# Gated mix of linear attention and a gated MLP: denominators in 128 rows, one output tile turned in place, weights and operands asked for at other points

## Chip, cores, metric

The kernel runs on one core of a Trainium2 chip. The metric is the device time of one execution in microseconds, the median of several runs. The core has five engines with instruction queues of their own: TensorE (PE; its weight loads are listed as PEld), VectorE (DVE), ScalarE (ACT), GpSimd (POOL) and SyncE (SP), which here only issues DMAs. ScalarE and GpSimd can issue DMAs too.

## What is computed

```python
x = A_x                                              # 1 x 2048 x 576
g = sigmoid((x * gate_w).sum(-1, keepdims=True))
# a: linear attention, 32 heads of 18
q, k, v = split(x @ wqkv)
phi_q = concat(softmax(q @ w_phi), softmax(-(q @ w_phi)))     # per head, 36 features
phi_k = the same of k
num = phi_q @ (phi_k^T v);  den = phi_q . sum(phi_k) + 1e-6
a = (num / den) @ wo
# b: gated MLP, 576 -> 4608 -> 576
b = (relu(x @ W_gate) * (x @ W_up)) @ W_down
out = g * a + (1 - g) * b
```

Everything is float32. Most products are done in three passes of a rounded type, high x high, high x low and low x high, so nearly every operand is split by ScalarE (the high part, a copy) and VectorE (the low part, a subtraction).

## The kernel before

The 2048 rows are 16 tiles of 128 (`t`), or 4 blocks of 512 (`TB`), handled in the order `BLOCKS` = 3, 0, 1, 2. So "block 0" of the text below is the first handled, and "block 3" holds tiles 8 to 11. The program is one function, `gated_mix_kernel`, with three stages.

1. Tiles: for each tile keys, queries, values and their softmax parts; `kv_step` sums keys times values. The softmax parts `e` of the queries are turned by TensorE (`turn_all`, L374) into 108-row operands. Tiles of the last block go straight into their operand buffer `PH`; the others are stored to a DRAM scratch `eT` and fetched a block at a time (`fetch`, L431). At the very start the loop at L219 loads five slices of `x` and `wv`.
2. Division and projection, a block `b` at a time: `sums(b, ...)` multiplies `PH` by the keys' sums (L556), ScalarE copies numerators to `R` and small DMAs gather denominators in `dn`; `invert(b)` takes the reciprocal times the gate and sends it by DMA to rows of `kt_`; `split_inverse(b)` splits it on GpSimd into `rd`; `divide(b, k)` spreads it over the rows of a head by a matmul with a 0/1 matrix (`spread`, L616), multiplies `R` and splits the result into `oh`, `ol`; `first_out` (block 0) or `project_out(b, m)` multiplies by `wo`, and `rows_out` stores to the DRAM scratch `att`. `dn`, `R` and the chain invert, DMA, split, divide exist once per block.
3. Main stage: 72 units (two halves of the rows, 36 column chunks of the MLP's weights), each of seven products (`product`, L1098) by a Strassen-like scheme. Operands `XO` are split copies of sums of `x`; each unit's weights are split by `blocks`, `sums_of_blocks`, `block_sums` in the first half and reloaded from DRAM in the second (`load_operands`, L883). The down products add into `ac` tiles that begin with `att` (`load_acc`), and are stored at the half's end (`store`, L1182). Around units 35 to 37 the operands are exchanged (`swap_in`).

`in_order` fixes the order of instructions on the engines it names to that of the program: TensorE, SyncE and GpSimd in stage 2, all engines in stage 3. In stage 2 a scheduler places VectorE's and ScalarE's instructions, apart from those inside `after(...)` or `behind()`, which must follow the ones named. A wait at the head of SyncE's or GpSimd's queue therefore holds all DMAs behind it.

Of the kernel before, what the change touches and what calls it, by code (L numbers as in the profile page):

```python
# [83 lines left out]
def gated_mix_kernel(  # L84
# [126 lines left out]
    with tc.tile_pool(name="ps_v", bufs=1, space=PSUM) as ps_v:  # L211
        pv = [[ps_v.tile([P, TB], F32, name=f"pv{2 * i + c}")[:, :VC[c][1]] for c in range(2)] for i in range(4)]

        warm = raw.tile([P, TB], F32R, name="warm", tag="raw")
        nc.vector.memset(warm.bitcast(F32), 0.0)
        for n in range(15):
            nc.tensor.matmul(pv[3][1], warm[:, :P], warm[:, :VC[1][1]], start=True, stop=True)
        xh, xl, x4 = x_tiles(0)
        for k in range(5):  # L219
            w = raw.tile([P, TB + VW], F32, name="xwv", tag="raw")  # L220
            nc.sync.dma_start(w[:, :TB], xT[:, k, :TB])
            nc.sync.dma_start(w[:, TB:], wv[:, k])
            if k < 4:
                split(xh[:, k], xl[:, k], w[:, :TB])
            else:
                split_x4(x4, w[:, :TB])
            split(wv_h[:, k, :VW], wv_l[:, k, :VW], w[:, TB:])
            for i in range(4):
                ts = slice(i * P, (i + 1) * P)
                for c, (v0, vn) in enumerate(VC):  # L230
                    cs = slice(v0, v0 + vn)
                    if k < 4:
                        ops = [(xh[:, k, ts], wv_h), (xh[:, k, ts], wv_l), (xl[:, k, ts], wv_h)]
                    else:
                        ops = [(x4[:, ts], wv_h), (x4[:, ts], wv_l)]
                    for n, (m, w_) in enumerate(ops):
                        nc.tensor.matmul(pv[i][c], m, w_[:, k, cs], start=k == 0 and n == 0,  # L237
                                         stop=k == 4 and n == 1)
# [131 lines left out]
    def turn_all(t, bb):  # L370
# [55 lines left out]

    def fetch(tb, queue=nc.sync):
        operands(tb)
        for i in range(4):
            t = 4 * tb + i  # L430
# [136 lines left out]

    RD, OW = [], {}

# [20 lines left out]
    def invert(b):  # L590
# [3 lines left out]
        tt(out=dn, in0=gT[:, BLOCKS[b] * P:(BLOCKS[b] + 1) * P], in1=dn, op=MULT)  # L594
        nc.sync.dma_start(kt_[2 * H * (b % 2):][:H, :TB], dn)

    def split_inverse(b):

        if not RD:
            RD.append(rb.tile([4 * H, TB], F32R, name="rd", bufs=1))  # L600
        i = 2 * H * (b % 2)
        d2, hi, lo = kt_[i:i + H, :TB], RD[0][i:i + H], RD[0][i + H:i + 2 * H]
        nc.gpsimd.tensor_copy(hi, d2)
        pt(out=lo, in0=d2, in1=hi.bitcast(F32), op=SUB)

    def divide(b, k):
# [7 lines left out]
        ps = kv_bank(1 - k % 2 if b > 1 or b == 1 and k < 2 else 0)  # L614
        half = slice(2 * H * (b % 2), 2 * H * (b % 2 + 1))
        nc.tensor.matmul(ps[:n], spread[half, k, :n], RD[0][half], start=True, stop=True)  # L616
        r = R[:n, k]
# [46 lines left out]
    with in_order(tc, nc, nc.tensor, nc.sync, nc.gpsimd):  # L664
# [75 lines left out]
        gather(1, 3, 2, 1, 0)  # L740
        split_inverse(1)
        with after(tc, nc, nc.vector, halves[1]):
            whole(final)
        first_out(3, range(5))
        two = pp.tile([P, 2, TB], F32, name="po", tag="pp")
        turn_all(FIRST - 1, [(2, turned(kv_bank(0))), (0, turned(two[:, 0])), (1, turned(two[:, 1]))])
        store_turned(FIRST - 1, nc.gpsimd)
        divide(0, 1)
# [4 lines left out]
    xo = ctx.enter_context(tc.tile_pool(name="xo", bufs=3, **L_))  # L753
    xr = ctx.enter_context(tc.tile_pool(name="xr", bufs=2, **L_))
    op_ = BS.enter_context(tc.tile_pool(name="op", bufs=2, **L_))
    tb_ = BS.enter_context(tc.tile_pool(name="tb", bufs=6, **L_))
    XO = {}
    def root_rows(tb):
# [5 lines left out]
    def rows_out(b, m, ps):  # L764
# [70 lines left out]

    RAW, WO = {}, {}
    units = [(0, c) for c in range(NC)] + [(1, (c - 2) % NC) for c in range(NC)]
# [40 lines left out]
    def load_operands(u):  # L878
# [6 lines left out]
        WO[u] = {1: (b, 0), 2: (b, 1), 4: (b, 2), 5: (o, 2), 6: (o, 0), 7: (o, 3), 3: (o, 1)}  # L885

    def early():
        for i in (5, 6):
# [40 lines left out]
    with in_order(tc, nc, nc.tensor, nc.sync, nc.gpsimd):  # L929
        x0, x1, x2 = (operand_ahead(i) for i in range(3))  # L930
        fetch(BLOCKS[3], nc.gpsimd)
        load_operand(0, 0, nc.gpsimd)
        load_operand(0, 1, nc.gpsimd)
        first_out(2, range(5))
        halves = two[:, 0], two[:, 1]
        sums(2, (4, 5), halves)
        divide(0, 0)
        first_out(1, range(5))
        sums(2, (3, 2), halves)
        for m in range(5):  # L940
            first_out(0, (m,))
            rows_out(0, m, PW[m])
            if m in (0, 1, 3):
                divide(1, (4, 3, None, 2)[m])
        sums(2, (1, 0), halves)
        gather(2, 4)
        invert(2)
        gather(2, 3, 2, 1, 0)
        split_inverse(2)
        divide(1, 1)  # L950
        divide(1, 0)
        for m in range(5):
# [4 lines left out]
            if m == 2:  # L957
                gather(3, 4)
                invert(3)
                gather(3, 3, 2, 1, 0)  # L960
                split_inverse(3)
                whole(x0)
            if m > 0:
                divide(2, 5 - m)
            if m in (0, 1):
                root_rows(m + 2)
            if m == 4:
                divide(2, 0)
                whole(x1)
        for m in range(5):  # L970
# [4 lines left out]
            if m == 1:  # L975
# [15 lines left out]
                load_rests(0, (6,))  # L991
        unit0, unit1 = unit(0), unit(1)
        for m in range(5):
            project_out(3, m)
            with behind():
                if m == 0:
                    next(unit0)
                if m == 1:
                    whole(unit0)
                if m == 2:  # L1000
                    next(unit1)
                if m == 3:
                    whole(unit1)
            if m in (1, 2):
# [15 lines left out]

    NG = NC // 2
    DOWN = (1, 5, 6, 3, 7, 2, 4)
    ADDS = {1: (0, 0), 5: (1, 1), 3: (0, 1), 6: (0, 1), 2: (0, 0), 7: (1, 1), 4: (1, 0)}
    WDR, WD, W4, HID, ACC, ACC4, BANK, REST = {}, {}, {}, {}, {}, {}, {}, {}

    def load_down(g):
        if g < 2 * NG:
            WDR[g] = wdp.tile([P, 9 * P], F32, name="wdr", bufs=1)  # L1030
            nc.sync.dma_start(WDR[g], wd[units[2 * g][1] // 2])

# [147 lines left out]
    def store(keys):  # L1180
        for hf, i, m, t in keys:
            nc.sync.dma_start(out[rows(i, m, t, hf)], ACC.pop((hf, i, m, t)))  # L1182
            if hf == 0:
                load_acc(1, i, m, t)

# [38 lines left out]
    def swap_in(u, j):  # L1224

        i = j + 7 * (u - NC + 1)
        if 2 <= i < 7:
            if i in (3, 4):
                load_rests(1, (2, 3, 4) if i == 3 else (5, 6))
            load_in_place(1, i)  # L1230
        if i in (1, 2):
            operand(1, i - 1)
        if 2 <= i - 4 < 7:
            low_in_place(1, i - 4)
        if 2 <= i - 3 < 7:
            high_in_place(1, i - 3)
        if 2 <= i - 5 < 7:
# [3 lines left out]
    done = []  # L1241

    def add_up():

        if PEND:
            done.extend(PEND.pop()())
        store(done)
        done.clear()

# [37 lines left out]
    def step(u, j):  # L1287
# [122 lines left out]
        if u == 0:  # L1410
            if j < 3:
                next(early, None)
            elif j < 5:
                plain_down(0, (high, low)[j - 3])
# [28 lines left out]

    later_half, early = second_half(), early()
    with in_order(tc, nc, nc.tensor, nc.vector, nc.scalar, nc.gpsimd, nc.sync):
        load_down(0)
        load_w(2)
        for u in range(len(units)):
# [89 lines left out]
def _layout(A_x, A_wqkv, A_w_phi, A_wo, B_W_gate, B_W_up, B_W_down, gate_w):  # L1538
# [32 lines left out]
    mask = np.zeros((QK, QG + 4), np.float32)  # L1571
    spread = np.zeros((4, H, 5, P), np.float32)
    for r in range(QK):
        h = r // (2 * DH)
# [3 lines left out]
    for k in range(5):  # L1578
        for r in range(P):
            spread[:, wo_rows[k * P + r] // DH, k, r] = 1.0  # L1580
    spread = spread.reshape(4 * H, 5, P)
# [19 lines left out]
```

## Time and profile before

| | |
|---|---|
| median of 3 runs | 1608.23 us (1607.2 to 1611.56) |
| profiled execution: its own time / span | 1607.92 us / 1605.9 us |
| mean granted TensorE clock | 0.997 |
| TensorE / VectorE / ScalarE / GpSimd busy | 98% / 74% / 35% / 11% |

Stage 2 lies at about 240 to 353 us of the span, the main stage after it; the halves change at about 980. Rows of the profile read: start in us, length in us, engine, line of the kernel, operation, tile written <- tiles read, shape, count, and in brackets the idle time before it with what ended it. "SPq" is SyncE's DMA queue.

### The profile page before, as it was taken

Reading aid. Unit: us, or ns where it says so; the run is one execution under the profiler, and the core shown is the slowest. Engines: PE = TensorE matmul, PEld = TensorE weight load, DVE = VectorE, ACT = ScalarE, POOL = GpSimd, SP = SyncE. Lnnn points to the kernel's source line nnn. Section 1 sums busy time; section 2 is a strip of 40 time slices with the busy share of each in tenths; the row PEclk is TensorE's granted clock in tenths of the full one; section 3 lists DMA queues with packets and bytes.
Section 4 is the critical chain, followed back from the end, with each engine's and each line's share of the span. In section 5 each row is a group of like instructions: output and inputs, shape, how many; then the busy total and the mean of one; then the engine's idle time right before and its main releaser. Section 6 shows DMA issues by size and latency. Waiting matters only on the chain.

```text
span 1605.9 us, 20175 instructions
## 1 busy us (share of the span) xinstructions
PE 1580.5 (98%) x7823; PEld 1314.5 (82%) x7823; DVE 1192.4 (74%) x1864; ACT 559.9 (35%) x918; POOL 171.3 (11%) x234
## 2 busy tenths in 40 slices
PE   9999999899999999999999999999999999999998
PEld 9899995577888888888888887788888888888887
DVE  4997775477787877878777777677776777767777
ACT  4444335463332332333333234223223232232331
POOL 0125522100000000000000002111111111111110
PEclk9999999999999999999999999999999999999999
DMA  5373415569655565655554525634344343443432
GB/s 165 108 242 134 162 41 148 177 234 351 215 220 212 217 249 217 222 218 189 214 197 172 208 83 175 242 129 183 134 151 181 129 174 143 148 184 129 169 148 74
DMA packets 65370, 284.59 MB, mean 177 GB/s; under 512 B 6842, under 2 KB 17338, under 8 KB 56572
## 3 DMA queue, kind: packets, MB, share of 16 engines
q1 hardware_dynamic: 62828, 273.30, 46.8%
q0 software_dynamic: 1872, 8.97, 1.8%
q8 instruction: 61, 1.00, 0.2%
q10 hardware_dynamic: 576, 1.05, 0.2%
q14 instruction: 33, 0.27, 0.0%
HBM read 172.67 MB, written 109.21 MB: 176 GB/s over the span
## 4 chain that ended last, share of the span: by engine, by line
PE 91%; DMA 3%; DVE 3%; ACT 1%; issue 1%; POOL 0%; SPq 0%; ACTq 0%; DVEq 0%; POOLq 0%
PE cx L1098 28%; PE ca L1098 13%; PE pd L1138 12%; PE pd L1161 10%; PE cy L1098 7%; PE kv L175 4%; PE pq L175 3%; PE pk L175 3%; PE pm L1138 2%; PE pm L1161 2%; PE kv L417 1%; DMA dn<-R 1%; PE ptr L374 1%; PE pv L237 1%; DMA wdr<-wd 1%; PE pw L175 1%
## 5 line engine op out<-in xcount | busy, mean ns | idle before, releaser
L1205 ACT ACTIVATE hh<-g 128x512 fp32r<-128x512 f32 x195 | 120.1, 624 | 459.1 <-DVE g L1255 289.8
L1176 DVE TENSOR_TENSOR ac<-pd,ac 128x512 f32<-128x512 f32 x238 | 164.0, 689 | 145.9 <-PE pd L1161 145.7
L1098 PE MATMUL cx<-xo,wb 128*128 128x512 f32 x1008 | 250.9, 392 | 5.0 <-DVE u L1380 3.5
L1098 PE MATMUL cx<-xo,ws 128*128 128x512 f32 x1008 | 252.4, 390 | 3.0 <-ACT g L1259 2.8
L1098 PE MATMUL ca<-xo,ws 128*128 128x512 f32 x1008 | 252.0, 389 | 0.6 <-DMA ws<-wsd 0.6
L1098 PEld LDWEIGHTS cx<-xo,wb 128*128 128x128 f32 x1008 | 189.2, 189 | 47.1 <-DVE u L1380 4.4
L1098 PEld LDWEIGHTS cx<-xo,ws 128*128 128x128 f32 x1008 | 188.9, 188 | 43.8 <-ACT g L1259 4.7
L1098 PEld LDWEIGHTS ca<-xo,ws 128*128 128x128 f32 x1008 | 189.1, 188 | 40.3 <-issue 1.0
L1138 PE MATMUL pd<-hh,wd 128*128 128x512 f32 x576 | 200.7, 389 | 0.0
L1161 PE MATMUL pd<-hh,wd 128*128 128x512 f32 x476 | 185.2, 389 | 0.0
L1144 DVE TENSOR_TENSOR ac<-pd,ac 128x512 f32<-128x512 f32 x144 | 99.1, 688 | 106.6 <-PE pd L1138 103.1
L1210 DVE TENSOR_TENSOR hl<-g,hh 128x512 fp32r<-128x512 f32 x195 | 136.4, 699 | 1.9 <-ACT hh L1205 0.2
L1259 ACT ACTIVATE g<-cx 128x512 f32<-128x512 f32 x144 | 84.9, 590 | 128.1 <-PE cx L1098 128.0
L1138 PEld LDWEIGHTS pd<-hh,wd 128*128 128x128 f32 x576 | 108.1, 188 | 22.6
L1098 PE MATMUL cy<-xo,wb 128*128 128x512 f32 x504 | 125.9, 389 | 0.0
L1061 ACT ACTIVATE wd<-wdr 128x384 fp32r<-128x384 f32 (+1 forms) x106 | 62.3, 606 | 152.9 <-DMA wdr<-wd 152.9
L1138 PE MATMUL pd<-hl,wd 128*128 128x512 f32 x288 | 112.2, 389 | 1.0 <-ACT xo L830 1.0
L1098 PEld LDWEIGHTS cy<-xo,wb 128*128 128x128 f32 x504 | 94.6, 188 | 19.6
L1161 PEld LDWEIGHTS pd<-hh,wd 128*128 128x128 f32 x476 | 89.4, 188 | 18.5
L1161 PE MATMUL pd<-hl,wd 128*128 128x512 f32 x238 | 92.6, 389 | 0.0
L814 POOL TENSOR_TENSOR xo<-xr,xo 32x512 fp32r<-32x512 f32 x5 | 8.2, 1637 | 653.9 <-DVE xo L814 646.1
L1064 DVE TENSOR_TENSOR wd<-wdr,wd 128x384 fp32r<-128x384 f32 (+1 forms) x106 | 69.3, 669 | 5.5 <-ACT wd L1061 5.5
(250 smaller groups left out, 2564.9 us busy)
## 6 DMA issues: line engine op xcount, KB each, us to landing
wsd<-ws SPq DMA_DIRECT2D x34, 1280.0 KB
ws<-wsd SPq DMA_DIRECT2D x34, 1280.0 KB
wbd<-wb SPq DMA_DIRECT2D x34, 960.0 KB
wb<-wbd SPq DMA_DIRECT2D x34, 960.0 KB
wr<-wgu SPq DMA_DIRECT2D x36, 768.0 KB
wdr<-wd SPq DMA_DIRECT2D x36, 576.0 KB
eT<-et SPq DMA_DIRECT2D x10, 594.0 KB
xt<-xb SPq DMA_DIRECT2D x7, 768.0 KB
```

What stands on the lines that cost most here:

```text
L175: nc.tensor.matmul(ps, w, m, start=i == 0, stop=i == len(pairs) - 1)
L237: nc.tensor.matmul(pv[i][c], m, w_[:, k, cs], start=k == 0 and n == 0, stop=k == 4 and n == 1)
L1061: nc.scalar.activation(o[:, 0], a, AF.Copy)
L1064: tt(out=o[:, 1], in0=a, in1=o[:, 0].bitcast(F32), op=SUB)
L1098: nc.tensor.matmul(ps, w, v, start=first and m == 0, stop=m == len(pairs) - 1, skip_group_check=True)
L1138: nc.tensor.matmul(ps, w, v, start=k == 0 and (i < 2 or first), stop=k == len(mms) - 1 and (i < 2 or last), skip_group_check=True)
L1144: tt(out=a, in0=ps, in1=a, op=ADD)
L1161: mm = lambda ps, w, v, a, z: nc.tensor.matmul(ps, w, v, start=a, stop=z, skip_group_check=True)
L1176: tt(out=a, in0=ps, in1=a, op=ADD)
L1205: nc.scalar.activation(h, src, AF.Copy)
L1210: tt(out=l, in0=src, in1=h.bitcast(F32), op=SUB)
L1259: nc.scalar.activation(a, ps, AF.Copy)
```

## The change

- **128 rows.** `spread` holds the heads' rows in its first 64 rows only, twice; the other 64 are zero. `rd` is two tiles, one for even and one for odd blocks, whose last 64 rows are set to zero; `divide` multiplies all 128 rows. The inverse of every block arrives in the same 32 rows of `kt_`.
- **Operand slots.** `R` of block 2 takes one of the three operand slots `xo`. Tile 11 (`FIRST - 1`) is turned straight into block 3's `PH`, so `fetch` of that block brings three tiles instead of four, and one store is gone.
- **Order in stage 2.** `split_inverse(1)` goes behind the start of the pools; the `sums` of block 2 are spread into `first_out`, before `rows_out(0, ...)`; `invert(2)` follows `divide(1, 0)`; two operand loads on GpSimd's queue follow `split_inverse(2)`; `invert(3)` and `split_inverse(3)` move one projection later, behind `divide(2, 1)`; `att` stores of blocks 2 and 3 are issued from GpSimd.
- **Main stage prepared earlier.** Down weights lie in a pool of their own (`wdrp`) and are first loaded in `project_out(2)`; units 0 and 1 are split from there on, unit 2's weights are loaded and the last two operands split in `project_out(3)`.
- **Middle and start.** `load_acc` of the second half runs three steps after the store of the same tile; the operand exchange loads its rests one step earlier and splits one step later. Two of the five `wv` slices are loaded from ScalarE's queue.

```diff
-            nc.sync.dma_start(w[:, TB:], wv[:, k])
+            (nc.scalar if k < 2 else nc.sync).dma_start(w[:, TB:], wv[:, k])
...
-            if t >= FIRST:
+            if t >= FIRST - 1:
                 o = PH[t // 4][:, t % 4]
...
-            RW[b] = rb.tile([P, 5, TB], F32, name="R")
+            RW[b] = xo.tile([P, 5, TB], F32, name="R", tag="xo") if b == 2 else rb.tile([P, 5, TB], F32, name="R")
...
-        nc.sync.dma_start(kt_[2 * H * (b % 2):][:H, :TB], dn)
+        nc.sync.dma_start(kt_[:H, :TB], dn)
...
-        i = 2 * H * (b % 2)
-        d2, hi, lo = kt_[i:i + H, :TB], RD[0][i:i + H], RD[0][i + H:i + 2 * H]
+        j = b % 2
+        if j not in RD:
+            RD[j] = (rd_ if j else rb).tile([4 * H, TB], F32R, name="rd", bufs=1)
+            nc.gpsimd.memset(RD[j][2 * H:].bitcast(F32), 0.0)
+        d2, hi, lo = kt_[:H, :TB], RD[j][:H], RD[j][H:2 * H]
...
-        nc.tensor.matmul(ps[:n], spread[half, k, :n], RD[0][half], start=True, stop=True)
+        nc.tensor.matmul(ps, spread[:, k], RD[b % 2], start=True, stop=True)
...
-        nc.sync.dma_start(att[m * P:m * P + n, BLOCKS[b] * TB:(BLOCKS[b] + 1) * TB], o)
+        (nc.gpsimd if b > 1 else nc.sync).dma_start(att[m * P:m * P + n, BLOCKS[b] * TB:(BLOCKS[b] + 1) * TB], o)
...
         x0, x1, x2 = (operand_ahead(i) for i in range(3))
-        fetch(BLOCKS[3], nc.gpsimd)
-        load_operand(0, 0, nc.gpsimd)
-        load_operand(0, 1, nc.gpsimd)
+        split_inverse(1)
+        fetch(BLOCKS[3], nc.gpsimd, 3)
         first_out(2, range(5))
         sums(2, (4, 5), halves)
         divide(0, 0)
-        first_out(1, range(5))
+        first_out(1, range(3))
         sums(2, (3, 2), halves)
+        first_out(1, range(3, 5))
+        sums(2, (1, 0), halves)
+        gather(2, 4)
         for m in range(5):
             first_out(0, (m,))
             rows_out(0, m, PW[m])
             if m in (0, 1, 3):
                 divide(1, (4, 3, None, 2)[m])
-        sums(2, (1, 0), halves)
-        gather(2, 4)
-        invert(2)
+        divide(1, 1)
+        divide(1, 0)
+        with after(tc, nc, nc.vector, last_of(nc, nc.vector)):
+            invert(2)
         gather(2, 3, 2, 1, 0)
         split_inverse(2)
-        divide(1, 1)
-        divide(1, 0)
+        load_operand(0, 0, nc.gpsimd)
+        load_operand(0, 1, nc.gpsimd)
         for m in range(5):
             project_out(1, m)
...
             if m == 2:
                 gather(3, 4)
-                invert(3)
+                whole(x0)
+            if m > 0:
+                for k in ((), (4,), (3,), (2, 1), (0,))[m]:
+                    divide(2, k)
+            if m in (0, 1):
+                root_rows(m + 2)
+            if m == 3:
+                with after(tc, nc, nc.vector, last_of(nc, nc.vector)):
+                    invert(3)
                 gather(3, 3, 2, 1, 0)
                 split_inverse(3)
-                whole(x0)
-            if m > 0:
-                divide(2, 5 - m)
-            if m in (0, 1):
-                root_rows(m + 2)
             if m == 4:
-                divide(2, 0)
                 whole(x1)
...
                 load_rests(0, (6,))
-        unit0, unit1 = unit(0), unit(1)
+                load_down(0)
+            if m > 1:
+                with behind():
+                    if m == 2:
+                        unit0, unit1 = unit(0), unit(1)
+                        next(unit0)
+                    if m == 3:
+                        whole(unit0)
+                    if m == 4:
+                        next(unit1)
+        load_w(2)
+        first = early()
         for m in range(5):
             project_out(3, m)
             with behind():
                 if m == 0:
-                    next(unit0)
-                if m == 1:
-                    whole(unit0)
-                if m == 2:
-                    next(unit1)
+                    whole(unit1)
                 if m == 3:
-                    whole(unit1)
+                    next(first)
+                if m == 4:
+                    next(first)
...
-            WDR[g] = wdp.tile([P, 9 * P], F32, name="wdr", bufs=1)
+            WDR[g] = wdrp.tile([P, 9 * P], F32, name="wdr")
...
-            if i in (3, 4):
-                load_rests(1, (2, 3, 4) if i == 3 else (5, 6))
+            if i in (2, 3):
+                load_rests(1, (2, 3, 4) if i == 2 else (5, 6))
...
-        if 2 <= i - 4 < 7:
-            low_in_place(1, i - 4)
-        if 2 <= i - 3 < 7:
-            high_in_place(1, i - 3)
+        if 2 <= i - 5 < 7:
+            low_in_place(1, i - 5)
+        if 2 <= i - 4 < 7:
+            high_in_place(1, i - 4)
...
     def add_up():
 
+        if len(STORED) > 2:
+            for hf, i, m, t in STORED.pop(0):
+                if hf == 0:
+                    load_acc(1, i, m, t)
         if PEND:
             done.extend(PEND.pop()())
         store(done)
+        STORED.append(tuple(done))
         done.clear()
```

More of the change, by code (lines that the diff above doesn't have):

```diff
@@ L425, in operands, with fetch @@
         PH[tb] = PP[BLOCKS.index(tb) % 2].tile([QK, 4, NQ, P], F32, name="ph")
-    def fetch(tb, queue=nc.sync):
-        operands(tb)
-        for i in range(4):
+    def fetch(tb, queue=nc.sync, n=4):
+        if tb not in PH:
+            operands(tb)
+        for i in range(n):
             t = 4 * tb + i
@@ L566, in sums @@
                 PH.pop(BLOCKS[b])
-    RD, OW = [], {}
+    RD, OW = {}, {}
     def gather(b, *kk):
@@ L1572, in _layout @@
     spread = np.zeros((4, H, 5, P), np.float32)
+    copies = spread[:2]
     for r in range(QK):
@@ L1579, in _layout @@
         for r in range(P):
-            spread[:, wo_rows[k * P + r] // DH, k, r] = 1.0
+            copies[:, wo_rows[k * P + r] // DH, k, r] = 1.0
     spread = spread.reshape(4 * H, 5, P)
```

31 lines of the change are left out of this document (12 added, 19 removed).

## The prediction

> **What bounds the kernel.** I read the page first, then a table of stretches, then TensorE's timeline inside the stretches that are not full.
>
> ```profile
> PE 1580.5 (98%) x7823; PEld 1314.5 (82%) x7823; DVE 1192.4 (74%) x1864; ACT 559.9 (35%) x918; POOL 171.3 (11%) x234
> ...
> 0.00:240.00 240.00, 235.63 (x1928) 225.97 (x1929) 184.45 (x291) 100.09 (x168) 72.11 (x53) 1.00 0.42 142
> 240.00:340.00 100.00, 93.27 (x398) 57.23 (x397) 52.56 (x87) 47.97 (x79) 17.20 (x23) 0.98 0.53 171
> 340.00:400.00 60.00, 55.44 (x233) 44.39 (x233) 45.16 (x65) 27.50 (x36) 0.00 (x0) 0.97 0.87 319
> 400.00:960.00 560.00, 560.00 (x2472) 463.70 (x2471) 437.27 (x659) 191.44 (x258) 0.00 (x0) 1.00 0.55 204
> 960.00:1040.00 80.00, 75.00 (x326) 60.42 (x325) 55.41 (x79) 29.45 (x50) 13.66 (x17) 1.00 0.58 199
> ```
>
> The first row is the page's busy time; the others are the table by stretch (TensorE's busy time is the first number after the stretch's length; the last three are granted clock, DMA share and GB/s). TensorE sets the time. From 400 to 960 it never stops, so nothing done there can matter. The change works in the stretches with holes: 6.7 us idle in 240 to 340, 4.6 in 340 to 400, 5.0 in 960 to 1040, a little at the start. The clock column shows a further loss: 0.98 and 0.97. What the change can win is these holes, that clock, and matmul time that is itself wasteful.
>
> **Denominators in 128 rows.** Timeline of TensorE around one and around two of the 20 `divide` matmuls (L616; start, length):
>
> ```profile
> 282.90 0.40 PE L633 MATMUL pw<-oh,wo 128*128 128x512 f32 x1
> 283.22 0.50 PE L616 MATMUL kv<-rd,spread 64*128 64x512 f32 x1
> 283.65 0.50 PE L633 MATMUL kv<-oh,wo 128*128 128x512 f32 x1
> 283.99 0.40 PE L633 MATMUL kv<-ol,wo 128*128 128x512 f32 x1
> 284.22 0.62 PE L633 MATMUL kv<-oh,wo 128*128 128x512 f32 x2
> ...
> 288.19 0.73 PE L616 MATMUL kv<-rd,spread 64*128 64x512 f32 x2
> 288.84 0.96 PE L175 MATMUL kv<-oh,wo 128*128 128x512 f32 x3
> ```
>
> Two 128-row matmuls of 512 columns start 0.23 apart (283.99 to 284.22). Around the 64-row one the steps are 0.32, 0.43 and 0.34: 1.09 where 0.69 would do, so 0.40 per change of shape and back. The 20 divides stand in about 15 groups; at six of them the neighbour is a 64-column `sums` matmul (L556), whose own change of shape stays, and I count 0.25 there: 9 x 0.40 + 6 x 0.25 = 5.1, taken as **-5.0** (between 0, if loading other weights costs it, and 6.0). The zeros cost nothing on TensorE: 512 columns pass in either case. Two memsets are added on GpSimd, of about the 0.60 that a cast of 512 elements takes there; it sits idle 12 and 17 us ahead of the casts shown below, and without that cover each would delay a divide by 0.6.
>
> The Trainium skill speaks against this edit: "TensorEngine Tiling (Array Packing)", Performance Considerations, advises two-fold row tiling when the contraction is 64 or less, as tiles of 64 rows can work at the same time. By that rule giving up 64 rows would gain nothing and might cost up to one matmul per pair. The row of the pair does not bear it out: two divides starting at 288.19 hold TensorE until 288.84, 0.33 each, slower than full matmuls, for both use the same 64 rows. The same page, Key Properties, says that a change of tiling mode drains TensorE; the 0.40 agrees.
>
> **Block 3's rows and the inverse of block 2.** Two waits of TensorE, and what led to them on the other engines:
>
> ```profile
> 282.37 0.56 POOL L431 DMA_DIRECT2D ph<-eT  x1 [2.71 <-DMA eT<-et]
> ...
> 293.41 1.90 PE L556 MATMUL po<-ph,kvm 108*64 108x512 f32 x6 [1.07 <-issue]
> ...
> 288.93 1.59 SPq L562 DMA_DIRECT2D dn<-R  x2
> ...
> 290.11 1.29 DVE L620 TENSOR_TENSOR ol<-R,oh 128x512 fp32r<-128x512 f32 x2
> ...
> 297.89 0.95 DVE L593 RECIPROCAL dn<-dn 128x128 f32<-128x128 f32 x1 [6.49 <-DMA R<-og]
> ...
> 299.24 0.63 SPq L595 DMA_DIRECT2D kt<-dn  x1
> ...
> 301.56 0.60 POOL L603 CAST rd<-kt 32x512 fp32r<-32x512 f32 x1 [17.53 <-DMA kt<-dn]
> ...
> 303.56 0.68 PE L616 MATMUL kv<-rd,spread 64*64 64x512 f32 x1 [2.58 <-POOL rd L604]
> ```
>
> Tile 11's turned rows go out to DRAM and come back; the fourth fetch is issued only at 282.37, and the first matmul on those rows (293.41) waits 1.07. Written straight into `ph`, one store and one fetch disappear and the three fetches that remain wait for no store: **-1.1**.
>
> Block 2's chain is reciprocal 297.89, DMA, cast, matmul 303.56: 5.67 from reciprocal to matmul. It starts late because the last `sums` of block 2 come after all of `first_out(0)`, their `dn` DMAs stand on SyncE's queue behind five `att` stores, and two operand loads on GpSimd's queue compete. All three orders are reversed: `sums(2, (1, 0))` moves up, the `att` stores fall behind, and `load_operand` (two issues on GpSimd, some 0.56 each like the fetch's) goes behind `split_inverse(2)`. The private slot for `R[2]` lets these sums run before `divide(0, 0)` frees the old one. The new reciprocal stands right behind `divide(1, 0)`'s last subtraction, 291.4 in today's times, so `rd` is ready at 291.4 + 5.7 = 297.1. TensorE has, from 288.84, two projections of 14 matmuls and two pairs of `sums` (1.90) ahead of that divide: 288.84 + 28 x 0.23 + 3.8 = 299.1, 2 us later, and both ends hang on the same divides. The wait goes: **-2.6**, and with it the slow clock after it, priced below at **-1.6**. In exchange VectorE becomes tight: block 1's five divides cost it two passes of 0.65 each, with the first result and one cast between some 7.7, while TensorE has left, from the first of them to the end of `project_out(1, 0)`, 12 + 4 + 14 matmuls, 6.9: **+1.0** (0 to 2). The loads moved behind `split_inverse(2)` are issued near 297; the first is wanted after one more divide, projection and pair, 299.1 + 0.2 + 3.2 + 1.9 = 304.4, so the 7 us between hide it.
>
> **Block 3's inverse.** Here the change delays something:
>
> ```profile
> 314.90 0.95 DVE L593 RECIPROCAL dn<-dn 128x128 f32<-128x128 f32 x1
> ...
> 319.30 1.47 POOL L603 CAST rd<-kt 32x512 fp32r<-32x512 f32 x1 [12.42 <-DMA kt<-dn]
> 320.85 1.79 POOL L604 TENSOR_TENSOR rd<-kt,rd 32x512 fp32r<-32x512 f32 x1
> ...
> 321.55 0.50 PE L175 MATMUL pw<-ol,wo 128*128 128x512 f32 x1 [0.24 <-DVE ol L620]
> ...
> 323.25 0.50 PE L175 MATMUL pw<-ol,wo 128*128 128x512 f32 x1 [0.74 <-DVE ol L620]
> ...
> 323.92 0.68 PE L616 MATMUL kv<-rd,spread 64*64 64x512 f32 x2
> ```
>
> Today reciprocal 314.90 leads to `rd` at 322.64 and the divide at 323.92: 1.3 to spare. The waits in front (0.24 and 0.74) are VectorE finishing block 2 late. In the new order the reciprocal follows `divide(2, 1)`'s last subtraction. From the end of `project_out(1, 3)` I count 3.1 us for these two divides (0.5 to the first result, four passes of 0.65), then 5.7 for the chain as it was for block 2, or 7.7 as it was here: 8.8 to 10.8. TensorE has two divides, 9 matmuls, one divide and 14 matmuls in that time: 26 x 0.23 = 6.0. So a new wait of 2.8 to 4.8 opens; it swallows the 1.0 of today's waits, and other passes of VectorE in between can shift it. Net **+2.0** (bounds -1.0, if the chain is as tight as today, and +5.0). Behind the waiting divide stand all of block 3's projections.
>
> **Start of the main stage.** TensorE at its first units:
>
> ```profile
> 360.80 1.88 PE L1098 MATMUL cx<-xo,ws 128*128 128x512 f32 x7 [0.91 <-ACT g L1259]
> ...
> 367.20 5.08 PE L1098 MATMUL cx<-xo,wb 128*128 128x512 f32 x14 [2.94 <-DVE u L1380]
> ...
> 380.81 3.51 PE L1098 MATMUL cx<-xo,wb 128*128 128x512 f32 x14 [0.58 <-DVE u L1380]
> ...
> 343.29 0.96 DVE L849 TENSOR_TENSOR wb<-wr,wb 128x768 fp32r<-128x768 f32 x1 [3.50 <-ACT wb L846]
> ```
>
> The granted clock of 0.97 over these 60 us (and 0.98 over the 100 before) is a loss of 1.8 and 2.0 us. VectorE is late: it still splits unit 1's weights and the last operands when units 0 and 1 want its sums. The same 14 matmuls take 5.08 after the 2.94 pause and 3.51 otherwise, so a pause of that length costs **1.6** more in slow clock. Units 0 and 1 now begin during `project_out(2)`, where VectorE stands idle (3.50 before 343.29 alone), the last two operands go into `project_out(3)`, and down weights and unit 2's raw weights are asked for before the stage. Backlog gone: 0.91 + 2.94 + 0.58 + 1.6 = **-6.0** (-3 to -6). The `att` stores of blocks 2 and 3, now on GpSimd, leave SyncE's queue free for these loads; GpSimd is 0.00 busy in 340 to 400.
>
> **The middle.** SyncE's longest waits and TensorE's stops between 960 and 1040:
>
> ```profile
> SPq L1106 <- DMA outT<-ac: 27.7, 8, 8.3
> ...
> 981.27 0.50 PE L1138 MATMUL pd<-hl,wd 128*128 128x512 f32 x1 [1.00 <-ACT xo L830]
> ...
> 1001.69 1.89 PE L1098 MATMUL cx<-xo,ws 128*128 128x512 f32 x7 [1.30 <-ACT g L1259]
> ...
> 1033.14 1.88 PE L1098 MATMUL cx<-xo,wb 128*128 128x512 f32 x7 [1.45 <-DMA wb<-wbd]
> ...
> 1036.33 1.86 PE L1098 MATMUL ca<-xo,ws 128*128 128x512 f32 x7 [0.62 <-DMA ws<-wsd]
> ...
> 1039.51 1.89 PE L1098 MATMUL cx<-xo,ws 128*128 128x512 f32 x7 [0.62 <-ACT g L1259]
> ```
>
> Each `load_acc` stands right behind the store of the same tile and blocks SyncE until it has landed: 27.7 us in eight waits, and the weight loads behind it come late. Three steps later the store has mostly landed. The splits moved one step later ease the first stop. 1.00 + 1.30 + 1.45 + 0.62 + 0.62 = 5.0; I take **-4.5** (-2.5 to -5), as splits and down weights still meet in one unit.
>
> **The first loads.**
>
> ```profile
> 1.65 0.43 SPq L222 DMA_DIRECT2D xwv<-wv  x1
> ...
> 5.73 0.69 ACT L148 ACTIVATE wv_h<-xwv 128x588 fp32r<-128x588 f32 x1 [1.26 <-DMA xwv<-wv]
> 6.48 1.84 PE L237 MATMUL pv<-wv_h,xh 128*128 128x294 f32 x6 [0.98 <-ACT wv_h L148]
> ```
>
> From ScalarE's queue `wv` can be asked for about 0.9 earlier (without the two issues, 0.43 each, ahead of it on SyncE's). TensorE's 0.98 is the most that this wait can return; I take **-0.5** (0 to -1.0; beyond it if the clock then rises sooner).
> The Trainium skill, "DMA: Bandwidth & Descriptors", Issuing engines are not separate DMA queues, says that a second issuing engine saves only the issue time; by that the term would be -0.4, and no run yet shows it.
>
> **Sum.** -0.5 -5.0 -1.1 -2.6 -1.6 +1.0 +2.0 -6.0 -4.5 = -18.3. The profiled execution took 1607.92 (span 1605.9 and 2.0 around it), 0.3 below the median 1608.23: 1607.92 - 18.3 = **1589.6 us**.
>
> **Rivals.**
> 1. *Block 3's inverse is the new stop.* At its bound of +5.0 the pause is as long as those of 2.58 and 2.94 that lowered the clock, so 3.0 + 1.6 more: 1594.2. For: the count above; against: today's order already makes VectorE late there. 0.20.
> 2. *The 128 rows do not do what they should*: the 0.40 belongs to something else, such as the weights. 5.0 come back: 1594.6. Against: 128-row matmuls change weights each time at 0.23. 0.14. (The tiling advice of the Trainium skill's "TensorEngine Tiling (Array Packing)", Performance Considerations, would give this time too.)
> 3. *Slower: operands land late.* Units 0 and 1 now stand ahead of other work in ScalarE's and VectorE's order, waiting for loads that are issued once `divide(3, 0)` is through. By the tile sizes 2.9 MB reach to the end of unit 1's weights and 4.5 MB to the last operand. TensorE needs them after 79 matmuls of the projections, 18 us, and after 9 more and six products of 7, 30 us. At 319 GB/s they take 9 and 14 us, at 171 17 and 26. At half of 171 the last operand comes 52 us after issue, 22 late: 1589.6 + 22 + 1.6 = 1613. It decides from under about 95 GB/s (47 us for the 4.5 MB, 17 late, the whole gain); the stretch moved 319. 0.06.
> 4. *No difference*: the holes reappear behind VectorE. It was 53% busy in 240 to 340: 0.04.
>
> The forecast has 0.50; 0.06 lies below 1584 (a clock that rises sooner at the start, block 3 at its good end).
>
> **Range and chances.** From 1583.5 (forecast less the good ends, 6 us) to 1599.0 (rivals 1 and 2 together): about 0.85 of the chance. A measurement tells 0.3%, 4.8 us, from no change. Faster 0.90, same 0.04, slower 0.06.
>
> **What would show it.** Right: divides 0.23 apart from their neighbours; no wait of `kv` for `rd` at block 2, a new one at block 3; clock 1.00 in the stretch with units 0 to 2; SyncE's wait of `ac` for `outT` under 8 us. Wrong: waits of `xo` or `wb` splits for DMA that reach TensorE, or a total above 1603.

## The result, and the profile after

The changed kernel takes **1595.38 us** (median; 1593.93 to 1595.84), the kernel before 1607.72 in the same comparison: ratio 0.9919, interval 0.9905 to 0.9934, 12.3 us faster. The profiled execution took 1595.61 with a span of 1593.5. The forecast was 1589.6, its range 1583.5 to 1599.0: faster, as predicted, but with two thirds of the expected gain.

The table by stretch of the changed kernel, with the columns of the prediction's first fence:

```profile
0.00:240.00 240.00, 235.55 (x1943) 225.96 (x1943) 185.71 (x298) 100.04 (x169) 72.62 (x54) 1.00 0.42 144
240.00:340.00 100.00, 91.59 (x393) 58.73 (x392) 53.08 (x85) 49.45 (x81) 17.96 (x27) 0.97 0.60 192
340.00:400.00 60.00, 57.16 (x250) 46.29 (x249) 45.69 (x65) 30.20 (x41) 2.75 (x5) 1.00 0.77 283
...
960.00:1040.00 80.00, 80.00 (x355) 66.06 (x354) 61.00 (x92) 27.85 (x50) 15.18 (x19) 1.00 0.62 212
```

The middle is full now (80.00 of 80), the main stage's start lost its slow clock (1.00) and some of its holes. But stage 2 (240 to 340) got *more* idle time, 8.4 us instead of 6.7, and its clock fell from 0.98 to 0.97. TensorE's timeline there, with VectorE, SyncE's queue and GpSimd between the waits:

```profile
291.71 1.93 PE L557 MATMUL po<-ph,kvm 108*64 108x512 f32 x6
...
299.24 0.50 PE L617 MATMUL kv<-rd,spread 128*128 128x512 f32 x1
...
313.49 0.94 DVE L594 RECIPROCAL dn<-dn 128x128 f32<-128x128 f32 x1
...
315.10 0.68 DVE L621 TENSOR_TENSOR ol<-R,oh 128x512 fp32r<-128x512 f32 x1
315.27 0.63 SPq L596 DMA_DIRECT2D kt<-dn  x1
...
315.83 0.50 PE L175 MATMUL pw<-ol,wo 128*128 128x512 f32 x1 [1.15 <-DVE ol L621]
...
317.58 0.60 POOL L605 CAST rd<-kt 32x512 fp32r<-32x512 f32 x1 [6.68 <-DMA kt<-dn]
...
319.57 1.22 PE L617 MATMUL kv<-rd,spread 128*128 128x512 f32 x2 [3.01 <-POOL rd L606]
```

The first two rows have lost their brackets: block 3's fetched rows (1.07 before) and block 2's inverse (2.58 before) are waited for no longer. The last row is the new stop: block 3's chain from reciprocal (313.49) to matmul (319.57) takes 6.1 us and TensorE stands still for 3.01 of them. The 1.15 in front of it belong to the same move: the reciprocal and two passes behind it now stand ahead of `divide(2, 0)`'s last subtraction (315.10), for which TensorE waits. Behind the pause the clock halves. The table by stretch, cut at the clock's own steps (third column from the end):

```profile
310.00:318.60 8.60, 5.40 (x22) 3.46 (x20) 7.53 (x12) 4.24 (x6) 1.47 (x3) 1.00 0.49 143
318.60:325.43 6.83, 5.86 (x14) 4.61 (x15) 2.66 (x4) 1.23 (x2) 1.43 (x2) 0.50 0.78 250
325.43:340.00 14.57, 14.01 (x62) 11.28 (x61) 9.71 (x15) 7.29 (x10) 2.19 (x4) 1.00 0.91 343
```

In these 6.83 us, 5.86 of matmul time ran at half speed; at full clock it would take half of that, so the slow clock cost 2.9, about as much as the wait itself.

To see where the time went, TensorE's run is cut at five marks: the first `divide` matmul, the first matmul of the main stage, of unit 3, of unit 30 and of unit 45 (49 matmuls a unit). Lengths in us, each from the starts in one profile of the kernel:

| | divide(0, 4) to main stage | main stage to unit 3 | unit 30 to unit 45 | median |
|---|---|---|---|---|
| before (second profile) | 94.92 (95.30) | 47.97 (47.97) | 264.56 (265.20) | 1607.72 |
| after | 93.71 | 44.30 | 258.02 | 1595.38 |
| inverse early (e2) | 88.39 | 44.30 | 258.03 | 1589.84 |
| block 3's divides late (e7) | 88.99 | 44.32 | 258.05 | 1589.94 |
| 64 rows (e1) | 95.57 | 44.30 | 258.10 | 1596.59 |
| inverse early, 64 rows (e10) | 90.33 | 44.38 | 258.04 | 1591.44 |
| preparation late (e4) | 93.32 | 48.00 | 258.05 | 1597.89 |
| units earlier still (e8) | 89.10 | 46.88 | 258.04 | 1592.77 |
| rests on GpSimd (e9) | 88.37 | 46.17 | 258.06 | 1592.10 |
| accumulators behind store (e3) | 92.20 | 44.30 | 263.43 | 1599.45 |
| exchange old (e6) | 92.75 | 44.31 | 259.35 | 1596.27 |
| wv on SyncE (e5) | 92.64 | 44.31 | 257.99 | 1593.72 |

Unit 3 to 30 (470.3) and unit 45 to the last matmul (465.3) are the same in before and after. Ahead of divide(0, 4) (258.04 before, 257.00 after) the profiles differ by chance, as the last experiment shows. A wait of that first divide for block 0's `rd` lies there too: 0.75 in the changed kernel's profile, 0.4 to 0.7 in e7, e8 and e10, none in the other profiles; whether the change brings it is open. In the first column chance counts as well: after, e3, e5 and e6 run the same instructions in that stretch and differ by up to 1.5, of which 1.2 is half clock (5.86 of matmul time at half speed in after, 3.41 in e3 and e5). The change's gain thus lies in three stretches: -1.2, -3.7 and -6.5.

### The profile page after: what moved, and what is told of

Read it like the earlier page. It is cut to its first block, busy times and chain, and to the rows that moved or that the text cites. A ratio compares the mean times of both kernels' runs of the same rounds, so it can differ in the third digit from the quotient of the medians.

```text
span 1593.5 us, 20181 instructions
## 1 busy us (share of the span) xinstructions
PE 1573.1 (99%) x7823; PEld 1313.6 (82%) x7823; DVE 1190.4 (75%) x1864; ACT 559.8 (35%) x918; POOL 175.3 (11%) x244
## 4 chain that ended last, share of the span: by engine, by line
PE 94%; DVE 2%; DMA 1%; ACT 1%; issue 1%; POOL 0%; SPq 0%; DVEq 0%; POOLq 0%; ACTq 0%
PE cx L1114 28%; PE ca L1114 14%; PE pd L1154 12%; PE pd L1177 10%; PE cy L1114 7%; PE kv L175 4%; PE pq L175 4%; PE pk L175 3%; PE pm L1154 2%; PE pm L1177 2%; PE kv L417 1%; PE ptr L374 1%; PE pw L175 1%; PE pv L237 1%; PE po L557 1%; DMA dn<-R 1%
```

## The experiments

All are single edits of the changed kernel unless it is said otherwise; each time is a median of four to twelve executions.

**e2: the late inverse undone.** Theory: block 3's inverse, moved one projection later, costs what is missing.

```diff
             if m == 2:
                 gather(3, 4)
+                invert(3)
+                gather(3, 3, 2, 1, 0)
+                split_inverse(3)
                 whole(x0)
...
-            if m == 3:
-                with after(tc, nc, nc.vector, last_of(nc, nc.vector)):
-                    invert(3)
-                gather(3, 3, 2, 1, 0)
-                split_inverse(3)
```

> The changed kernel with one thing put back: invert(3), its gathers and split_inverse(3) stand again one projection earlier, ahead of divide(2, 3), with no order forced on VectorE. Theory (the late inverse of block 3 makes TensorE wait 3.0 us for rd and 1.15 us before it, and the slow clock after it costs 3.4): the wait for rd falls under 1 us, the clock stays at 1.00, and the time falls by 4 to 6 us, to 1589.5 to 1591.5. Rival (VectorE is the limit there, so an early reciprocal only delays block 2's last subtractions by as much): within 1.5 us of 1595.4.

1589.84 (1589.06 to 1592.13), ratio 0.989 (0.9877 to 0.9904). TensorE's waits from 300 to 400 (total us, times, longest):

```profile
PE cx L1112 <- DVE u L1399: 2.9, 2, 1.8
PE kv L617 <- DVE R L619: 1.3, 2, 0.8
PE pw L175 <- DVE ol L621: 0.6, 1, 0.6
PE pw L175 <- ACT oh L620: 0.4, 1, 0.4
```

No wait for `rd`, full clock from 5 to the last microseconds, and the stretch to the main stage 5.3 shorter. This one move of the change costs 5.5 us by the medians.

**e7: the same wait, covered instead.** The inverse stays late, and all of block 3's divides go behind `project_out(2, 1)`, so that 14 more matmuls lie in front.

```diff
-            if m == 0:
-                divide(3, 4)
-                divide(3, 3)
             if m == 1:
-                for k in (2, 1, 0):
+                for k in (4, 3, 2, 1, 0):
                     divide(3, k)
```

> The changed kernel with block 3's five divides all behind project_out(2, 1) instead of two ahead of it. Theory (TensorE only needs 3.2 us of other work while rd of block 3 is made): no wait for rd, no slow clock, 5 to 6.5 us less: 1589 to 1590.5. Rival (the five divides then crowd VectorE and the weights' loads start later, so the wait moves to project_out(3) or to the main stage): 1592 to 1595.

1589.94 (1588.71 to 1591.1), ratio 0.9887 (0.9872 to 0.9902). The 1.15 for `ol` stays (1.14 here), the wait for `rd` and the slow clock are gone: 

```profile
316.06 0.50 PE L175 MATMUL pw<-ol,wo 128*128 128x512 f32 x1 [1.14 <-DVE ol L621]
...
319.86 0.73 PE L617 MATMUL kv<-rd,spread 128*128 128x512 f32 x2
```

Two different edits that share only the vanished wait give the same time: the wait with its slow clock is the cause, not the position of VectorE's passes. e2 and e7 are the fastest kernels of this study, 5.5 and 5.4 us under the changed one.

**e1 and e10: 64 rows again**, once in the changed kernel, once with the inverse early (e10), where no wait for `rd` can swallow a gain.

```diff
-        nc.tensor.matmul(ps, spread[:, k], RD[b % 2], start=True, stop=True)
+        nc.tensor.matmul(ps[:n], spread[:2 * H, k, :n], RD[b % 2][:2 * H], start=True, stop=True)
```

> The changed kernel, but divide multiplies only the 64 rows of rd and spread that hold data (and 64 columns for the last slice), as before; nothing else differs. Theory (a change of shape costs 0.40 us of TensorE per group of divides): the steps of 0.32, 0.43 and 0.34 us around a divide come back, and the time rises by 3 to 5 us, to 1598.5 to 1600.5. Rival (the 128 rows are worth nothing, the gain lies elsewhere): 1595.4, unchanged.

> The inverse of block 3 early, with 64-row denominators. Theory (the prediction's 5.0 for the 128 rows was too large because most divides have a 64-column neighbour or stand where VectorE holds TensorE up anyway; it does not hang on the wait for rd): 1.2 to 2.5 slower than with 128 rows, 1591 to 1592.4. Rival (the wait for rd at block 3 hid the gain in the run with 64 rows that came out at 1596.6): 4 to 5 slower, 1594 to 1595.

e1: 1596.59 (1596.15 to 1598.14), ratio 0.9932 (0.9919 to 0.9944), only 1.2 above the changed kernel, where 3 to 5 were expected. e10: 1591.44 (1591.01 to 1594.31), 1.6 above e2, with runs that overlap. In the stretch to the main stage the profiles say 1.9 both times (95.57 - 93.71, 90.33 - 88.39); the second pair, at full clock throughout, is the safer one. So the rival for e10, a gain hidden by the wait for `rd`, falls. TensorE around divide(1, 3) in the changed kernel, then in e1:

```profile
283.43 0.40 PE L634 MATMUL pw<-oh,wo 128*128 128x512 f32 x1
283.66 0.39 PE L617 MATMUL kv<-rd,spread 128*128 128x512 f32 x1
283.89 0.39 PE L634 MATMUL kv<-oh,wo 128*128 128x512 f32 x1
284.12 0.40 PE L634 MATMUL kv<-ol,wo 128*128 128x512 f32 x1
```

```profile
282.61 0.40 PE L634 MATMUL pw<-oh,wo 128*128 128x512 f32 x1
282.94 0.49 PE L617 MATMUL kv<-rd,spread 64*128 64x512 f32 x1
283.36 0.50 PE L634 MATMUL kv<-oh,wo 128*128 128x512 f32 x1
283.70 0.40 PE L634 MATMUL kv<-ol,wo 128*128 128x512 f32 x1
```

Steps of 0.23, 0.23, 0.23 against 0.33, 0.42, 0.34: the 0.40 per group holds. That the change of shape is its cause is not shown in full: two 64-row divides in a row, with no change between them, also start 0.33 apart (e1, at 308.83). It is the count that was wrong. Of the 15 groups, by their steps in e10 against e2, six gain 0.3 to 0.4; three next to a 64-column matmul gain 0.1 to 0.2; five gain nothing, one between two 64-column matmuls and four with a wait for VectorE or ScalarE close by; and divide(2, 0) loses 0.4, as it comes sooner and waits longer for `R`. That adds up to 2.3, of which 1.9 arrives.

**e4: preparation at the old points.**

```diff
-            if m > 1:
-                with behind():
-                    if m == 2:
-                        unit0, unit1 = unit(0), unit(1)
-                        next(unit0)
...
-        load_w(2)
-        first = early()
+        unit0, unit1 = unit(0), unit(1)
...
+        load_down(0)
+        load_w(2)
```

> The changed kernel with units 0 and 1, unit 2's raw weights, the last two operands and the first down weights prepared at the points where the kernel before prepared them. Theory (VectorE's backlog at the first units was worth 3.7 us, the step between the start of the main stage and unit 3): the pauses ahead of cx grow back from 1.26 and 1.17 to about 2.9 and 0.6, a half-clock window of 3.41 comes with them, 1598.5 to 1600. Rival (the backlog only moved into the projections of block 3, and what was won there came from the stage ahead): 1595 to 1596.5, with no new pause above 1.5.

1597.89 (1596.84 to 1600.37), ratio 0.9941 (0.9928 to 0.9955): 2.5 slower by the medians, a little under the lower end of what was expected; 3.7 longer in its own stretch (48.00 against 44.30). The pauses are those of before, to 0.01 us, and a half-clock window of 3.41 comes with them:

```profile
364.24 5.06 PE L1105 MATMUL cx<-xo,wb 128*128 128x512 f32 x14 [2.94 <-DVE u L1392]
...
377.84 3.47 PE L1105 MATMUL cx<-xo,wb 128*128 128x512 f32 x14 [0.58 <-DVE u L1392]
```

In the changed kernel the same places read so (TensorE and VectorE):

```profile
354.46 1.88 PE L1114 MATMUL cx<-xo,ws 128*128 128x512 f32 x7 [0.41 <-ACT g L1280]
...
358.97 0.68 DVE L816 TENSOR_TENSOR xo<-xr,xo 32x512 fp32r<-32x512 f32 x1
...
360.29 1.41 DVE L1080 TENSOR_TENSOR wd<-wdr,wd 128x1024 fp32r<-128x1024 f32 x2
...
361.62 0.68 DVE L1401 TENSOR_TENSOR u<-cx,u 128x512 f32<-128x512 f32 x1
...
362.36 3.48 PE L1114 MATMUL cx<-xo,wb 128*128 128x512 f32 x14 [1.26 <-DVE u L1401]
...
374.93 3.47 PE L1114 MATMUL cx<-xo,wb 128*128 128x512 f32 x14 [1.17 <-DVE u L1401]
```

VectorE's backlog is shorter but not gone: the last operand's split ends at 359.65, a `g` and the down weights' split follow, and `u` comes 1.26 late. 2.84 of the old 4.43 of pauses remain; 1.59 went, and the slow clock with them.

**e8: units one projection earlier still**, with the inverse early.

```diff
-            if m > 1:
+            if m > 0:
                 with behind():
-                    if m == 2:
+                    if m == 1:
                         unit0, unit1 = unit(0), unit(1)
                         next(unit0)
...
-            if m in (1, 2):
-                in_place(m + 2)
+            if m in (0, 1):
+                in_place(m + 3)
```

> The inverse of block 3 early (as in the run with 1589.84), and units 0 and 1 and the last operands prepared one projection earlier still. Theory (with the wait for rd gone, the 2.9 us that TensorE stands still for VectorE's sums at units 0 and 1 are the largest loss left, and VectorE has idle time from 327 on): 1586.8 to 1588.2, the two pauses under 1 us together. Rival (the raw weights have not landed by then, ScalarE waits for them and holds the rows of block 2, so the pause moves into the projections): 1589.5 to 1592.

1592.77 (1590.65 to 1593.44): 2.9 *slower* than e2. The theory fell, and not quite as the rival had it: ScalarE did not wait for weights. Its row ahead of unit 0's split shows that it was still placed behind the next tile of output rows, no earlier than before, while the operands' copies moved in between:

```profile
329.37 0.60 ACT L771 ACTIVATE o<-kv 128x512 f32<-128x512 f32 x1 [2.06 <-PE kv L175]
...
329.86 1.16 ACT L849 ACTIVATE wb<-wr 128x1152 fp32r<-128x1152 f32 x1
...
358.56 4.82 PE L1112 MATMUL cx<-xo,wb 128*128 128x512 f32 x14 [2.93 <-DVE u L1399]
```

The pause at unit 0 grew from 1.8 to 2.93, which brought a half-clock window back (358.02 to 361.43). In stage 2 a line further up in the program is a request to the scheduler, not an order.

**e9: the rests split on GpSimd**, again with the inverse early.

```diff
-            low_rest(0, i, tt)
+            low_rest(0, i, pt)
```

> The inverse of block 3 early, and the 32-row rests of the last four operands split on GpSimd instead of VectorE: four passes of 0.68 leave VectorE between 345 and 353, just ahead of the sums u for which TensorE waits 1.8 and 1.2. Theory (VectorE's queue of splits sets those two pauses): both go to nearly nothing, 1586.8 to 1588.2. Rival (the copies on ScalarE set them, or GpSimd's passes come too late): 1589 to 1591, pauses as before.

1592.10 (1590.85 to 1592.68), 2.3 slower than e2. Four passes left VectorE, and yet `u` of unit 0 came at 356.74, where e2 had it at 355.49. VectorE and GpSimd side by side, and TensorE after them:

```profile
338.65 1.57 POOL L816 TENSOR_TENSOR xo<-xr,xo 32x512 fp32r<-32x512 f32 x1 [0.60 <-ACT xo L832]
...
339.11 1.53 DVE L870 TENSOR_TENSOR wr<-wr 128x384 f32<-128x384 f32 x1
...
340.68 0.56 DVE L871 TENSOR_TENSOR wr<-wr 128x384 f32<-128x384 f32 x1
...
346.91 4.56 DVE L836 TENSOR_TENSOR xo<-xo 128x1024 fp32r<-128x1024 f32 x3
...
349.63 2.54 PE L1112 MATMUL cx<-xo,ws 128*128 128x512 f32 x7 [1.84 <-ACT g L1278]
...
370.50 3.51 PE L1112 MATMUL cx<-xo,wb 128*128 128x512 f32 x14 [1.48 <-DVE u L1399]
```

The pass at 339.11, which takes 0.56 in e2, takes 1.53 with a GpSimd pass over it, and ends 0.42 after that one: VectorE stands still until GpSimd is through. The delay passes on to ScalarE (its copy to `g` for unit 0 starts at 348.98, in e2 at 347.15), and a new stop of 1.84 opens at unit 0, with a half-clock window (350.62 to 354.03). The Trainium skill, "SBUF — State Buffer", Who interferes with whom, describes a port pair of these two engines as an exclusive lock; these rows agree.

**e3 and e6: the middle, in its two parts.** e3 loads the accumulators right behind the store again, e6 puts the operand exchange at its old points.

```diff
             nc.sync.dma_start(out[rows(i, m, t, hf)], ACC.pop((hf, i, m, t)))
+            if hf == 0:
+                load_acc(1, i, m, t)
```

```diff
-            if i in (2, 3):
-                load_rests(1, (2, 3, 4) if i == 2 else (5, 6))
+            if i in (3, 4):
+                load_rests(1, (2, 3, 4) if i == 3 else (5, 6))
...
-            low_in_place(1, i - 5)
+            low_in_place(1, i - 4)
...
-            high_in_place(1, i - 4)
+            high_in_place(1, i - 3)
```

> The changed kernel with load_acc again right behind the store of the same tile; the operand exchange keeps its new timing. Theory (the wait at the head of SyncE's queue made the weights late): SyncE's wait of ac for outT returns to over 20 us, TensorE's stops between 960 and 1030 return but for the first of 1.0, and the time rises by 4 to 5.5 us, to 1599.4 to 1601. Rival (the exchange's timing alone removed the stops): 1595.4 to 1596.5.

> The changed kernel with the operand exchange in the middle at its old points (rests one step later, splits one step earlier), the load of the accumulators still three steps behind the store. Theory (the exchange gave what the accumulators did not, 6.5 less 4.1): 1597.5 to 1598, a stop of about 1.0 for a split of xo near 975 and one or two behind it. Rival (the accumulators' late load alone frees the middle, and the splits wait for nothing then): 1595 to 1596, no stop.

e3: 1599.45 (1598.75 to 1600.6), 4.1 slower; 5.4 in its stretch. e6: 1596.27 (1595.2 to 1597.81), 0.9 slower; 1.3 in its stretch. SyncE's wait from 930 to 1050 (total us, times, longest) in the changed kernel and in e3, then the first two of four stops of TensorE between 960 and 1040 in e3, and the only one in e6:

```profile
SPq L1122 <- DMA outT<-ac: 5.1, 2, 3.3
```

```profile
SPq L1122 <- DMA outT<-ac: 28.2, 8, 7.4
```

```profile
992.50 1.88 PE L1114 MATMUL cx<-xo,ws 128*128 128x512 f32 x7 [1.70 <-ACT g L1277]
...
1023.65 1.89 PE L1114 MATMUL cx<-xo,wb 128*128 128x512 f32 x7 [1.17 <-DMA wb<-wbd]
```

```profile
973.57 0.50 PE L1154 MATMUL pd<-hl,wd 128*128 128x512 f32 x1 [1.00 <-ACT xo L832]
```

Each part brings back its own stops and no others: 5.4 + 1.3 = 6.7, close to the 6.5 of the stretch. (By the medians it is 5.0, but e6's runs overlap with the changed kernel's.) e6 came out between theory and rival: the 1.0 stop is real, more is not behind it.

**e5 and e11: the start.** e5 loads all `wv` slices from SyncE's queue again; e11 is the kernel before, unchanged, profiled once more.

```diff
-            (nc.scalar if k < 2 else nc.sync).dma_start(w[:, TB:], wv[:, k])
+            nc.sync.dma_start(w[:, TB:], wv[:, k])
```

> The changed kernel with all five slices of wv loaded from SyncE's queue, as before. Theory (the shorter first pause lets the full clock come at 4.6 instead of 10.0, and that is what gave 1.9 us ahead of the first sums): full clock again near 10, 1597 to 1597.5. Rival (only the issue time of two loads was saved, and the early clock has another reason): full clock stays near 5, 1595.6 to 1596.

> The kernel before, unchanged, for a second profile of its start. Theory (the chip's clock is raised in windows of 3.41 whose phase differs from execution to execution, and the late full clock of the first profile was such a phase): full clock between 4.5 and 7.5, first sums up to 1.9 earlier than 243.4, time as before. Rival (the loads of wv at SyncE's queue make the first pause long enough to deny the clock every time): full clock near 10 again, first sums at 243.4.

e5: 1593.72 (1593.68 to 1595.56), not slower than the changed kernel, so the theory falls; its full clock came at 5.49. It is 1.7 faster by the medians, as much as one half-clock window at block 3 is worth (its profile has one, 3.41 long, the changed kernel's two); that this is the reason is not shown. e11: 1608.39 (1604.31 to 1609.49), ratio 1.0003 (0.9993 to 1.0012). First `wv` matmuls of e11 and of the changed kernel:

```profile
5.70 1.08 PE L237 MATMUL pv<-wv_h,xh 128*128 128x294 f32 x6 [0.25 <-ACT wv_h L148]
```

```profile
5.83 0.54 PE L237 MATMUL pv<-wv_h,xh 128*128 128x294 f32 x2 [0.69 <-ACT xh L148]
```

The second profile of before pauses 0.25 where the first paused 0.98, reaches full clock at 5.25 instead of 10.04 and is at divide(0, 4) at 256.19 instead of 258.04. e10 reached full clock only at 10.33. So the start differs by chance: the first divide begins between 256.07 (e1) and 259.19 (e10) in profiles with the same instructions ahead of it. The edit of the loads does nothing that shows; in the changed kernel TensorE waits for a slice of `x` (`xh` in the bracket) instead of one of `wv`.

## Why the prediction came out as it did

The direction and the three places were right. By its steps, with the stretches of the first profile of before:

| step | predicted | measured | from |
|---|---|---|---|
| first loads | -0.5 | 0 | e5, e11 |
| 128 rows | -5.0 | -1.9 (medians: 1.2 and 1.6) | e1, e10 |
| fetch, inverse of block 2, its slow clock, tight VectorE | -4.3 | -4.6 | the rest of -1.2 |
| block 3's inverse | +2.0 | +5.3 (medians 5.5 and 5.4) | e2, e7 |
| main-stage start | -6.0 | -3.7 | e4 |
| middle | -4.5 | -6.5 | e3, e6 |
| sum | -18.3 | -11.4 | |

The -4.6 is what is left over; no run measures it alone. The two profiles lie 12.4 apart at the last matmul; the other 1.0 lies ahead of the first divide, where chance alone makes up to 3.

**Right.** Block 2's and the fetch's waits vanished, VectorE became tight at `project_out(1, 0)` (TensorE waits 0.53 and 0.22 there), and a wait of 2.8 to 4.8 was foretold at block 3: it is 3.01. GpSimd's att stores and the moved loads left no wait of TensorE's. The fall of SyncE's wait below 8 us (5.1) and of the main stage's slow clock came as said.

**The step that failed first: block 3's inverse.** It was netted at +2.0 on two assumptions: that the new wait swallows the 1.0 of VectorE's waits in front, and that the slow clock comes only at the bound of +5.0. Neither held. The wait for `ol` did not go but became 1.15, since the reciprocal and two passes behind it now stand ahead of block 2's last subtraction, and the clock halved for 6.83 us after a 3.01 pause, which cost 2.9. The prediction's own row of before, 2.58 with a slow window behind it, priced this, and even the shortest wait that it foretold, 2.8, was longer; the row was used for the gain at block 2 and not for the like loss at block 3. That is rival 1, at 1594.2 within 1.2 of the result. So close a hit is luck in part: its step is 6.6 (2.0 + 3.0 + 1.6) where 5.3 were measured, and the errors below cancel some of the rest.

**128 rows: the term was mis-sized.** The price per group, 0.40, was right; multiplying it by all groups was not. A group saves it only where TensorE's issue sets the pace. At divides that wait, or stand two matmuls ahead of a wait, for `R`, `oh` or `ol`, the saving becomes waiting. Rows for this stood in the timeline of the kernel before:

```profile
261.23 1.20 PE L633 MATMUL pw<-oh,wo 128*128 128x512 f32 x4 [0.45 <-DVE oh L620]
...
282.33 0.50 PE L633 MATMUL pw<-oh,wo 128*128 128x512 f32 x1 [0.41 <-ACT o L769]
```

They follow divide(0, 3) and divide(1, 4); each pause takes in the change of shape. Rival 2 (nothing gained) is wrong too: 1.9 of 5.0 came.

**Main-stage start: taken at its good end** (bounds -3 to -6). "Backlog gone" was an assumption; e4 and the changed kernel's rows show that over half of the pauses remained. Rivals 3 and 4 did not come about: no pause at the first units names a DMA.

**Middle: too small**, as -4.5 kept a reserve for splits and down weights in one unit. No stop remained. The stops' time, 5.0, understates them: undoing the two edits brings back 6.7. A stop here cost about 0.3 more than its bracket: one of 1.00 cost 1.33 (e6), four of 4.14 together 5.41 (e3), five of 4.99 together 6.54 (before).

The two errors at stage 2 (+3.1 and +3.3), the one at the main stage (+2.3) and the first loads (+0.5) outweigh the middle (-2.0) and the small one at block 2 (-0.3). The half clock at block 3 lasted one window in some profiles (e3, e5: 3.41) and two in others (after, e1, e4, e6: 6.83) after pauses of 3.0 to 3.1; the last section says on what that hung.

## What to carry to other kernels

Price a pause of the matmul engine as wait plus slow clock, for every new wait as for every removed one, and ask of a chain moved later where the matmuls are that cover it (e7: 14 of them were worth 5.4 us). A saving per instruction counts only at places where that engine's own issue sets the pace; go through the places one by one before multiplying. Where a DMA waits at the head of a shared queue for another one's landing, moving it a few steps later can return more than the stops that it visibly causes.

## What the runs showed of the hardware

- Half clock comes in windows of 3.41 us on a fixed grid: full clock in the changed kernel lasts 314.03 from its start to the first half window, 92 such windows. What counted was the time without a matmul inside one window. With each of the thirteen profiles cut into such windows from the start of its full clock, a window at full clock with 1.84 or more without a matmul was followed by one at half clock all 14 times, and one with 1.77 or less never. A half window with 0.97 or more was followed by a second one (after, e1, e4, e6), one with 0.54 or less by full clock. So 3.01 cost two windows in the changed kernel, where the pause reaches into the half window, and one in e3, where it ends with the window before; 1.84 cost one in e9 and 1.77 none in e2. The grid lies elsewhere in every execution. Two windows of the changed kernel, then one of e2 and one of e9 (TensorE's busy time is the first number after the length, the clock the third from the end):

```profile
315.19:318.60 3.41, 0.73 (x2) 0.30 (x2) 2.40 (x3) 0.60 (x1) 0.94 (x2) 1.00 0.15 45
318.60:322.01 3.41, 2.44 (x6) 1.96 (x7) 1.51 (x3) 0.89 (x2) 1.43 (x2) 0.50 0.62 115
...
353.18:356.59 3.41, 1.64 (x8) 1.05 (x7) 3.38 (x6) 0.00 (x0) 0.00 (x0) 1.00 1.01 426
...
347.21:350.62 3.41, 1.57 (x7) 1.01 (x6) 3.41 (x3) 2.83 (x5) 2.05 (x1) 1.00 0.98 370
```

- The Trainium skill, "TensorE: Matmul & The Clock Gate", What's actually happening, gives a free-running window of 3413 ns; the windows above agree.
- The Trainium skill, "TensorE: Matmul & The Clock Gate", Why this matters for your kernels, allows pauses of up to about 3 us. Here shorter ones (2.58, 1.84) were followed by a half window, so it is no safe limit.
- A VectorE pass under a GpSimd pass took 1.53 instead of 0.56 (e9).
